# Preparing the first attention layer: loads of x, the first value product and the order of the pieces

## The chip, the cores and the metric

The kernel runs on one core of a Trainium2 chip. The metric is the device time of one execution in microseconds. TensorE (PE) multiplies, VectorE (DVE), ScalarE (ACT) and GpSimd (POOL) do element-wise work, and SyncE (SP) issues all DMA transfers of this kernel in the order of its queue.

## The reference

Four layers work in turn on one x of 2048 rows and 640 columns, in float32: attention, Fourier mixing, attention, Fourier mixing. Cut to what matters here:

```python
def attention(x, wqkv, wo):                      # H = 32 heads of 20, window W = 256
    q, k, v = split(x @ wqkv)                    # each (H, S, 20)
    scores = einsum("bhqd,bhkd->bhqk", q, k) * 20 ** -0.5
    mask = (i - j >= 0) & (i - j < 256)
    p = softmax(where(mask, scores, -1e9))
    return merge(einsum("bhqk,bhkd->bhqd", p, v)) @ wo

x = x + attention(layernorm(x), wqkv, wo)
x = x + real_fourier(layernorm(x))
x = x + attention(layernorm(x), wqkv, wo)
x = x + real_fourier(layernorm(x))
```

## The kernel before

Every float32 product is made of three products of rounded operands: each operand is split into a high half (a rounding copy, on ScalarE) and a low half (the rest, a subtraction on VectorE or GpSimd), and high x high, high x low and low x high are added up in PSUM. `split` makes the two halves and `all3` issues the three products for each of the five blocks of 128 columns (KC = 5).

The change is in `before_heads`, which prepares an attention layer before the loop over the heads. It works on 16 tiles of 128 rows of x, four tiles to a block (`sb`). For tile t:

- `prep_load` issues the load of the tile (320 KB) on SyncE. In layer 0 the tiles 0 to 11 go to eight places in `tmp`, tiles 12 and later to the rotating buffers of `raw`.
- `prep_stats` computes mean and variance on VectorE, and 1/sqrt on GpSimd.
- `prep_norm` normalizes the tile in place on VectorE.
- `prep_turn` makes five transposes on PE (four into a bank of role x4, the fifth into role x1, which has one bank), and splits what comes out, from PSUM, into high (ScalarE) and low (VectorE) halves in `xnt`.
- `value(t)` makes the value product of the tile: two halves of 320 columns, each 15 products, copied by ScalarE and VectorE into a buffer `vst`, which is stored to DRAM for each pair of tiles.

`prep` does, for a running number r, the load of a tile ahead, the statistics of r + 2, the normalization of r + 1 and the turn of r. It is called once in each `value` and in some of the `pieces`.

`load_w` loads one of the five blocks of the value weights and splits it; `split_w(n)` runs n steps of these, two to a weight. `pieces(sb)` computes two pieces (chunks of 128 query and key columns, 15 products of 512 columns each) for a block and stores them in DRAM (`qk_d`). `packed(sb)` issues the 12 loads that bring the queries and keys of the first four heads back in the layout of the heads. `values(sb)` is four calls of `value`.

What sets the order is the order of the Python code: each engine runs its instructions in the order in which they are issued there, and waits only for data and buffers. Nothing plans. The same holds for SyncE, on which a store that waits for its data holds up each load behind it. The layers 0 and 2 share the code; `first` marks layer 0.

In layer 0 the order on PE is, with V for a value product, P for a piece's 15 products and T for the turn of a tile: T0 T1 V0 T2 V1 T3 V2 T4 V3 T5 T6 P T7 and so on: two pieces of block 0 and two of block 1, then V4 to V7, pieces of block 2, V8 to V11, pieces of block 3, V12 to V15. After that the heads start, on line 553.

Of the kernel before, what the change touches and what calls it, by code (L numbers as in the profile page):

```python
# [17 lines left out]
P = 128  # L18
S = 2048
D = 640  # L20
KC = D // P
# [33 lines left out]
def cuts(ap, n):  # L55

    return [ap[:, i:i + n] for i in range(0, ap.shape[1] - n + 1, n)]


def pairs(c):  # L60
    return [(c[2 * i], c[2 * i + 1]) for i in range(len(c) // 2)]


class Net:
    def __init__(self, nc, tc, ctx, a):
        self.nc, self.tc, self.a = nc, tc, a
        const = ctx.enter_context(tc.tile_pool(name="const", bufs=1))
        self.ln = ctx.enter_context(tc.tile_pool(name="ln", bufs=5))
        self.slots = ctx.enter_context(tc.tile_pool(name="slots", bufs=1))
        psum = ctx.enter_context(tc.tile_pool(name="psum", bufs=1, space=PSUM))  # L70
        self.work = ctx.enter_context(tc.tile_pool(name="work", bufs=2))
        dram = ctx.enter_context(tc.tile_pool(name="dram", bufs=1, space=DRAM))

        self.banks = psum.tile([P, 8, 512], F32, name="banks")

        def fixed(name, cols, dt):
            return const.tile([P, cols], dt, name=name)

        self.ident = fixed("ident", P, F32)
        nc.sync.dma_start(self.ident, a["ident"])  # L80
        self.mask = fixed("mask", 384, BF16)
        self.ones = const.tile([1, 128], F32, name="ones")
        nc.vector.memset(self.ones, 1.0)
        self.half = fixed("half", 1, F32)
        nc.vector.memset(self.half, -0.5)
        self.big, self.home = [None] * 4, [0, 1, 2, 3]
        self.qp, self.kp = [None] * 2, [None] * 2

        self.qk = dram.tile([2, 2 * D, S], F32, name="qk_d")
        self.vd = dram.tile([NQ, P, NB, 96], F32, name="v_d")  # L90
        self.ud = dram.tile([2, KC, P, S], F32, name="u_d")
        self.od = dram.tile([H, 32, S], F32, name="o_d")
        self.rd = dram.tile([NSB, H, 512], F32, name="r_d")
        self.td = dram.tile([2, KC, P, D], F32, name="t_d")
        self.xs = [dram.tile([S, D], F32, name=f"x_d{i}") for i in range(3)]
        self.turn = {}
        self.xn = {}
        self.ready, self.hid = 0, False
        self.slot = None
        self.posted = {}  # L100
        self.heavy = []
        self.left = 0
        self.tmp = None
# [27 lines left out]
    def next(self, name):  # L131
        i = self.turn.get(name, 0)
        self.turn[name] = i + 1
        tiles = getattr(self, name)[:3]
        return tiles[i % len(tiles)]
# [164 lines left out]
    def before_heads(self, xsrc):  # L300
        nc, a = self.nc, self.a
        self.proj = self.project()
        ready = self.ready
        first = ready == 0
        vst = [t.rearrange("p (q t c) -> p q t c", t=2, c=96) for t in self.pt[:2]]
        for v in self.pt[:2]:
            (nc.vector if first else nc.gpsimd).memset(v, 1.0)
        if first:
            self.take_tmp()
        if first:  # L310
            for t in range(3):
                self.prep_load(xsrc, t)
        state = [ready, ready + (6 if first else 4)]
        wv = pairs(cuts(self.kp[1], D) + cuts(self.qp[1], D))[:KC]
        spare = (cuts(self.pt[2], D) + cuts(self.pt[3], D) if first else [None] * 4) + [None]
        wl = [self.load_w(wv, a["wv"], [k], at=k, eng=nc.vector if first and k > 2 else nc.gpsimd, into=spare[k])
              for k in range(KC)]
        for f in wl:
            next(f)
        if first:  # L320
            for t in range(3, 6):
                self.prep_load(xsrc, t)
                if t < 5:
                    self.load_chunk(t - 3)
            mask = self.raw()[:, :384]
            nc.sync.dma_start(mask, a["mask"])
        if first:
            self.prep_stats(0)
        self.prep_stats(ready + 1)
        if first:  # L330
            self.prep_norm(0)

        def prep():
            r = state[0]
            if state[1] < r + 5:
                self.prep_load(xsrc, state[1])
                state[1] += 1
            self.prep_stats(r + 2)
            self.prep_norm(r + 1)
            self.prep_turn(r)  # L340
            state[0] += 1

        def split_w(n):
            for _ in range(n):
                if wl and next(wl[0], 1) is not None:
                    wl.pop(0)

        def pieces(sb):
            for c in range(2):
                if first and sb == 0:  # L350
                    prep()
                self.piece(c, sb, "q")
                split_w(4)
                if ready or sb and state[0] < 4 * sb + 8:
                    prep()

        def value(t):
            v, xt = vst[t // 2 % 2], self.xnt(t // 4)
            rs = slice((t % 4) * P, (t % 4 + 1) * P)
            ps = []  # L360
            for hf in range(2):
                p = self.bank("v", 320)
                cs = slice(hf * 320, (hf + 1) * 320)
                self.all3(p, [((xt[:, 0, k, rs], xt[:, 1, k, rs]), (wv[k][0][:, cs], wv[k][1][:, cs]))
                              for k in range(KC)])
                ps.append(p)
            prep()
            for hf in range(2):
                dst = v[:, 4 * hf:4 * hf + 4, t % 2, 0:84].rearrange("p q (h c) -> p q h c", c=21)[:, :, :, 1:21]
                src = ps[hf].rearrange("p (q h c) -> p q h c", q=4, h=4)  # L370
                if hf == 0:
                    nc.scalar.activation(dst, src, AF.Copy)
                else:
                    nc.vector.tensor_copy(dst, src)  # L374
            if t % 2:
                nc.sync.dma_start(self.vd[:, :, t - 1:t + 1, :].rearrange("q p t c -> p q (t c)"),
                                  v.rearrange("p q t c -> p q (t c)"))

        def values(sb):
            for f in wl:  # L380
                for _ in f:
                    pass
            for i in range(4):
                value(4 * sb + i)

        def packed(sb):
            for f in self.pack(0, sb):
                f()

        if first:  # L390
            split_w(4)
            prep()
            split_w(6)
            prep()
            for t in range(4):
                if t in (1, 2):
                    self.cut_chunk(t - 1)
                value(t)
            nc.gpsimd.tensor_copy(self.mask, mask)
            pieces(0)  # L400
            pieces(1)
        else:
            pieces(0)
            pieces(1)
            values(0)
        self.take_qk("kp", 0)
        self.ones_rows(0)
        packed(0)
        packed(1)
        values(1)  # L410
        pieces(2)
        self.load_chunk(2)
        packed(2)
        values(2)
        pieces(3)
        self.cut_chunk(2)
        self.load_chunk(3)
        packed(3)
        values(3)
        self.ones_rows(1)  # L420
# [1309 lines left out]
```

## Time and profile before

| | |
|---|---|
| median of three runs | 2174.63 us (2174.54 to 2177.93) |
| the profiled execution | 2173.64 us |
| its span | 2171.9 us |
| first transpose on PE | 7.96 us after the span's start |
| first product of the heads on PE | 125.02 us |
| PE busy in the first 125 us | 112.06 us |

Times in the timeline count from the start of the span. A row of it gives start, duration, engine, line, operation, the tiles written and read, their form, and how many instructions in a row it stands for; in brackets is the idle time ahead of it and what ended it. Tiles are named by their buffers: `big` holds x tiles at first (the `tmp` places) and normalized, turned x; `kp` and `qp` hold the split value weights for a time; `pt` the raw weights 0 to 3 and the value buffers.

### The profile page before, as it was taken

Reading aid. Unit: us, or ns where it says so; the run is one execution under the profiler, and the core shown is the slowest. Engines: PE = TensorE matmul, PEld = TensorE weight load, DVE = VectorE, ACT = ScalarE, POOL = GpSimd, SP = SyncE. Lnnn points to the kernel's source line nnn. Section 1 sums busy time; section 2 is a strip of 40 time slices with the busy share of each in tenths; the row PEclk is TensorE's granted clock in tenths of the full one; section 3 lists DMA queues with packets and bytes.
Section 4 is the critical chain, followed back from the end, with each engine's and each line's share of the span. In section 5 each row is a group of like instructions: output and inputs, shape, how many; then the busy total and the mean of one; then the engine's idle time right before and its main releaser. Section 6 shows DMA issues by size and latency. Waiting matters only on the chain.

```text
span 2171.9 us, 49261 instructions
## 1 busy us (share of the span) xinstructions
PE 2116.4 (97%) x17893; PEld 1768.5 (81%) x17893; DVE 1611.6 (74%) x3933; ACT 1167.9 (54%) x2611; POOL 932.6 (43%) x1458
## 2 busy tenths in 40 slices
PE   7999999899999999999999999998999999999999
PEld 7987777687878888889999877776777788888899
DVE  6348888786897968787751578887768878688777
ACT  3117887766554545543431288786665545455522
POOL 3037777876514224230230477777754333242300
PEclk9999999999999999999999999999999999999999
DMA  5546666786435353657646466667853454546653
GB/s 184 177 146 198 203 190 212 218 233 200 135 122 180 132 187 126 224 196 258 214 140 189 152 201 187 207 193 224 233 184 130 130 189 136 165 148 218 221 176 125
DMA packets 221619, 395.41 MB, mean 182 GB/s; under 512 B 39360, under 2 KB 85952, under 8 KB 221376
## 3 DMA queue, kind: packets, MB, share of 16 engines
q1 hardware_dynamic: 221376, 392.26, 57.0%
q8 instruction: 141, 2.31, 0.5%
q14 instruction: 102, 0.84, 0.1%
HBM read 273.94 MB, written 117.05 MB: 180 GB/s over the span
## 4 chain that ended last, share of the span: by engine, by line
PE 81%; DVE 6%; POOL 4%; ACT 4%; DMA 3%; issue 2%; SPq 0%; ACTq 0%; POOLq 0%; DVEq 0%
PE banks L1269 27%; PE banks L173 14%; PE banks L191 13%; PE banks L613 8%; PE banks L1524 6%; PE banks L583 6%; PE banks L553 4%; POOL ou L1199 1%; POOL big L166 1%; DVE qp L166 1%; ACT big L931 1%; PE banks L273 1%; PE banks L565 1%; POOL rs L981 1%; ACT big L160 1%
## 5 line engine op out<-in xcount | busy, mean ns | idle before, releaser
L558 DVE CUSTOM_DVE_ANT_0 banks<-banks,mask 128x384 f32<-128x384 f32 (+2 forms) x1024 | 525.5, 559 | 153.4 <-PE banks L553 117.5
L592 ACT ACTIVATE pt<-banks 128x384 f32<-128x384 f32 (+2 forms) x1024 | 430.1, 472 | 139.8 <-PE banks L553 59.5
L583 PE MATMUL banks<-qp,kp 61*128 61x384 f32 (+2 forms) x1024 | 302.8, 365 | 9.7 <-DMA qp<-mt 7.7
L598 POOL TENSOR_SCALAR_AFFINE_SELECT pt<-pt 128x256 f32<-128x256 f32 x512 | 213.5, 418 | 174.9 <-ACT pt L592 128.4
L553 PE MATMUL banks<-kp,qp 60*128 60x384 f32 (+2 forms) x1024 | 279.1, 359 | 4.8 <-DVE mc L558 4.5
L191 PE MATMUL banks<-big,wc 64*128 64x512 f32 x1920 | 272.1, 394 | 0.4 <-DVE pt L374 0.4
L583 PEld LDWEIGHTS banks<-qp,kp 61*128 61x128 f32 x1024 | 176.8, 185 | 68.0 <-issue 27.4
L613 PE MATMUL banks<-pt,vq 128*32 128x128 f32 x5760 | 215.3, 277 | 4.4 <-POOL pt L598 4.4
L191 PEld LDWEIGHTS banks<-big,wc 64*128 64x128 f32 x1920 | 183.3, 185 | 29.1 <-ACT x L477 6.7
L613 PEld LDWEIGHTS banks<-pt,vq 128*32 128x32 f32 x5760 | 144.3, 109 | 65.2 <-issue 48.2
L1199 POOL TENSOR_TENSOR pt<-pt,pt 128x512 f32<-128x512 f32 x36 | 62.8, 1744 | 293.0 <-DMA pt<-c 188.3
L602 POOL TENSOR_SCALAR_AFFINE_SELECT pt<-pt 128x256 f32<-128x256 f32 x448 | 187.4, 418 | 0.0
L553 PEld LDWEIGHTS banks<-kp,qp 60*128 60x128 f32 x1024 | 163.7, 185 | 26.7 <-DVE mc L558 16.3
L160 ACT ACTIVATE c<-pt 128x512 fp32r<-128x512 f32 x150 | 93.5, 626 | 151.0 <-POOL pt L1175 52.4
L160 ACT ACTIVATE qp<-pt 128x512 fp32r<-128x512 f32 (+1 forms) x195 | 119.9, 624 | 92.2 <-DVE pt L1200 38.9
L166 DVE TENSOR_TENSOR c<-pt,c 128x512 fp32r<-128x512 f32 x150 | 125.0, 843 | 52.0 <-ACT c L160 49.8
L166 DVE TENSOR_TENSOR qp<-pt,qp 128x512 fp32r<-128x512 f32 (+1 forms) x195 | 150.2, 783 | 12.4 <-ACT qp L160 9.8
L1269 PE MATMUL banks<-qp,big 128*128 128x512 f32 x630 | 151.2, 391 | 4.9 <-DVE qp L166 3.9
L558 DVE DVE_READ_ACCUMULATOR2_ANT mc<- 128x1 f32 x1024 | 145.2, 142 | 0.0
L1269 PEld LDWEIGHTS banks<-qp,big 128*128 128x128 f32 x630 | 117.0, 188 | 31.0 <-DVE qp L166 5.6
L1269 PE MATMUL banks<-qp,xc 128*128 128x512 f32 x480 | 117.9, 390 | 1.5 <-DVE xc L166 1.2
L1269 PEld LDWEIGHTS banks<-qp,xc 128*128 128x128 f32 x480 | 89.8, 188 | 21.9 <-DVE xc L166 2.1
(224 smaller groups left out, 4388.6 us busy)
## 6 DMA issues: line engine op xcount, KB each, us to landing
pt<-c SPq DMA_DIRECT2D x188, 512.0 KB
qk_d<-c SPq DMA_DIRECT2D x80, 512.0 KB
kp<-qk_d SPq DMA_DIRECT2D x384, 80.0 KB
qp<-qk_d SPq DMA_DIRECT2D x384, 80.0 KB
kp<-u_d SPq DMA_DIRECT2D x32, 640.0 KB
o_d<-ou SPq DMA_DIRECT2D x64, 256.0 KB
x_d<-x SPq DMA_DIRECT2D x48, 320.0 KB
v_d<-pt SPq DMA_DIRECT2D x16, 768.0 KB
```

The lines of the kernel that those rows point to most:

```text
L160: nc.scalar.activation(hi, src, AF.Copy, scale=-1.0 if neg else 1.0)
L166: (eng or nc.vector).tensor_tensor(out=lo, in0=src, in1=hi.bitcast(F32), op=OP.subtract)
L173: self.nc.tensor.matmul(p, x, y, start=n == 0, stop=n == last)
L191: self.nc.tensor.matmul(ps[a], x[r], y[r], start=half + i == 0, stop=half == 1 and i == n - 1, skip_group_check=True)
L553: nc.tensor.matmul(p, qp[quad % 2][b:b + 60, z, qb * P:(qb + 1) * P], kp[quad % 2][b:b + 60, z, k0 * P:(qb + 1) * P], start=True, stop=True)
L558: nc.vector.tensor_tensor_reduce(out=p, in0=p, in1=self.mask[:, 384 - n * P:], scale=1.0, scalar=NEG, op0=OP.add, op1=OP.max, accum_out=mc ...
L583: nc.tensor.matmul(self.banks[:, tb[e], :n * P], kp[quad % 2][b:b + 61, z, kb * P:(kb + 1) * P], qp[quad % 2][b:b + 61, z, kb * P:(kb + n) ...
L592: nc.scalar.activation(pt[quad, kb][:, 2 * z + e, :n * P], self.banks[:, tb[e], :n * P], AF.Exp, scale=SCALE)
L598: nc.gpsimd.affine_select(out=t[:, :, 0:P], in_=t[:, :, 0:P], pattern=[[0, 2], [1, P]], compare_op=OP.is_ge, fill=0.0, base=0, channel_mul ...
L602: nc.gpsimd.affine_select(out=t[:, :, 256:384], in_=t[:, :, 256:384], pattern=[[0, 2], [-1, P]], compare_op=OP.is_gt, fill=0.0, base=0, ch ...
L613: nc.tensor.matmul(p[32 * h:32 * h + 32, :], vq[:, 96 * (kb % 4) + 21 * h:96 * (kb % 4) + 21 * h + 32], t[:, h, (qb - kb) * P:(qb - kb + 1 ...
L1269: nc.tensor.matmul(self.banks[:, bk, :], p, b[q], start=start and m == 0, stop=stop and last and m == 2, skip_group_check=True)
```

## The change

In layer 0, `before_heads` is written in another order:

- Tile 0 of x is loaded first, then the identity for the transposes, the five weights, and tiles 1 to 7, with the two chunks of query and key weights and the mask between them. Before, tiles 0 to 2 stood ahead of the weights. `prep` now loads tile r + 6 (before, r + 4 at most), so the load of a tile stands further ahead in SyncE's queue.
- The low halves of all five value weights are made on VectorE. Before, those of weights 0 to 2 were made on GpSimd.
- A new function `opening` takes the place of the first steps: statistics, normalization and turn of tile 0 with the weights' splits between them, and the normalization of tile 1.
- A new function `first_value` makes the first value product: for each of the five blocks k it issues the three products of both halves, where `all3` makes one half through all blocks and then the other. The turn of tile 1 stands in it ahead of block 3.
- The turn of tile r then stands behind V r-1, one step later than before, up to V3. The first two pieces have no call of `prep` ahead of them any more.
- Pieces of block 1 come after V4 to V7, and V8 to V11 come ahead of the pieces of block 2.

The diff:

```diff
-        nc.sync.dma_start(self.ident, a["ident"])
@@ before_heads
         if first:
-            for t in range(3):
-                self.prep_load(xsrc, t)
-        state = [ready, ready + (6 if first else 4)]
+            self.prep_load(xsrc, 0)
+            nc.sync.dma_start(self.ident, a["ident"])
+        state = [2, 8] if first else [ready, ready + 4]
...
-        wl = [self.load_w(wv, a["wv"], [k], at=k, eng=nc.vector if first and k > 2 else nc.gpsimd, into=spare[k])
+        wl = [self.load_w(wv, a["wv"], [k], at=k, eng=nc.vector if first else nc.gpsimd, into=spare[k])
               for k in range(KC)]
...
         if first:
-            for t in range(3, 6):
+            for t in range(1, 8):
                 self.prep_load(xsrc, t)
-                if t < 5:
-                    self.load_chunk(t - 3)
-            mask = self.raw()[:, :384]
-            nc.sync.dma_start(mask, a["mask"])
-        if first:
-            self.prep_stats(0)
-        self.prep_stats(ready + 1)
-        if first:
-            self.prep_norm(0)
+                if t in (3, 5):
+                    self.load_chunk(t // 2 - 1)
+                if t == 4:
+                    mask = self.raw()[:, :384]
+                    nc.sync.dma_start(mask, a["mask"])
+        else:
+            self.prep_stats(ready + 1)
@@ prep
-            if state[1] < r + 5:
+            if state[1] < r + (8 if first else 5):
@@ pieces
-                if first and sb == 0:
-                    prep()
                 self.piece(c, sb, "q")
                 split_w(4)
-                if ready or sb and state[0] < 4 * sb + 8:
+                if ready or state[0] < 4 * sb + 9:
                     prep()
+        def opening():
+            self.prep_stats(0)
+            self.prep_norm(0)
+            split_w(6)
+            self.prep_turn(0)
+            self.prep_stats(1)
+            split_w(2)
+            self.prep_norm(1)
+            split_w(2)
+
+        def first_value(ps):
+            xt = self.xnt(0)
+            for k in range(KC):
+                if k == 3:
+                    self.prep_turn(1)
+                for hf, p in enumerate(ps):
+                    cs = slice(hf * 320, (hf + 1) * 320)
+                    for a, b in ((0, 0), (0, 1), (1, 0)):
+                        nc.tensor.matmul(p, xt[:, a, k, :P], wv[k][b][:, cs], start=k + a + b == 0,
+                                         stop=k == KC - 1 and a == 1)
+            self.prep_stats(2)
+            self.prep_norm(2)
+            self.prep_stats(3)
@@ value
-            prep()
+                prep()
+            else:
+                first_value(ps)
@@ the end of before_heads
         if first:
-            split_w(4)
-            prep()
-            split_w(6)
-            prep()
+            opening()
             for t in range(4):
                 if t in (1, 2):
                     self.cut_chunk(t - 1)
                 value(t)
             nc.gpsimd.tensor_copy(self.mask, mask)
             pieces(0)
-            pieces(1)
...
         packed(0)
-        packed(1)
-        values(1)
+        if first:
+            values(1)
+            pieces(1)
+            packed(1)
+            values(2)
+        else:
+            packed(1)
+            values(1)
         pieces(2)
...
-        values(2)
+        if not first:
+            values(2)
         pieces(3)
```

How the instructions move, on PE from the first transposes to the second value product. L273 and L272 are the transposes of an x tile, five to a turn, L173 and L172 value products out of `all3`, L370 those of `first_value`; `kp` holds weights 0 to 2, `qp` weights 3 and 4. Before:

```order
L273 MATMUL banks<-ident,big_108 128x128 x10
L173 MATMUL banks<-kp_103,big_157 128x320 x9
L173 MATMUL banks<-qp_104,big_157 128x320 x6
L173 MATMUL banks<-kp_103,big_157 128x320 x9
L173 MATMUL banks<-qp_104,big_157 128x320 x6
L273 MATMUL banks<-ident,big_108 128x128 x5
```

Now:

```order
L272 MATMUL banks<-ident,big_107 128x128 x5
L370 MATMUL banks<-kp_102,big_144 128x320 x18
L272 MATMUL banks<-ident,big_107 128x128 x5
L370 MATMUL banks<-qp_103,big_144 128x320 x12
L172 MATMUL banks<-kp_102,big_144 128x320 x9
L172 MATMUL banks<-qp_103,big_144 128x320 x6
```

The second turn has moved into the first value product, behind its first 18 products, and the third turn from before the second value product to behind it.

On VectorE, the opening: L218 and L217 with the two lines after them are a tile's statistics, L236 and L235 a normalization, L166 and L165 low halves, out of `pt` or `x` those of a weight, out of `banks` those of a turned tile. Before, after the two fills:

```order
L218 BN_STATS st<-big_108 128x6 x2
L220 BN_AGGR mv<-st 128x2
L222 TENSOR_SCALAR rs<-mv 128x1
L218 BN_STATS st<-big_108 128x6 x2
L220 BN_AGGR mv<-st 128x2
L222 TENSOR_SCALAR rs<-mv 128x1
L236 TENSOR_SCALAR big_108<-big_108,mv,rs 128x640
```

Now:

```order
L217 BN_STATS st<-big_107 128x6 x2
L219 BN_AGGR mv<-st 128x2
L221 TENSOR_SCALAR rs<-mv 128x1
L235 TENSOR_SCALAR big_107<-big_107,mv,rs 128x640
L165 TENSOR_TENSOR kp_102<-pt_95,kp_102 128x640 x2
L165 TENSOR_TENSOR kp_102<-pt_96,kp_102 128x640
L165 TENSOR_TENSOR big_144<-banks,big_144 128x4x128
L165 TENSOR_TENSOR big_144<-banks,big_144 128x128
```

The normalization of tile 0 has moved ahead of the statistics of tile 1, and three weights' low halves stand between it and tile 0's own low half.

On SyncE, the queue around the first loads of queries and keys (L250 and L249 are loads of x, L456 and L479 piece stores, L424 and L447 the rows of ones, L510 and L533 the loads of `packed`). Before:

```order
L456 DMA qk_d<-c 128x2x512
L250 DMA x<-x 128x640
L424 DMA kp_560<-ones 1x32x128 x2
L510 DMA kp_560<-qk_d 20x2x512 x6
L510 DMA qp_105<-qk_d 20x2x512 x6
L510 DMA kp_560<-qk_d 20x2x512 x6
L510 DMA qp_105<-qk_d 20x2x512 x6
L250 DMA x<-x 128x640 x2
```

Now:

```order
L479 DMA qk_d<-c 128x2x512
L249 DMA x<-x 128x640
L447 DMA kp_465<-ones 1x32x128 x2
L533 DMA kp_465<-qk_d 20x2x512 x6
L533 DMA qp_104<-qk_d 20x2x512 x6
L249 DMA x<-x 128x640 x2
```

The two loads of x behind the queries and keys are tiles 14 and 15 before and 13 and 14 now, and twelve loads fewer stand ahead of them; block 1's twelve come later, behind its pieces.

More of the change, by code (lines that the diff above doesn't have):

```diff
@@ L359, in value @@
             rs = slice((t % 4) * P, (t % 4 + 1) * P)
[L360 to L366, printed above, removed]
-            prep()
+            ps = [self.bank("v", 320) for _ in range(2)]
+            if t or not first:
+                for hf, p in enumerate(ps):
+                    cs = slice(hf * 320, (hf + 1) * 320)
+                    self.all3(p, [((xt[:, 0, k, rs], xt[:, 1, k, rs]), (wv[k][0][:, cs], wv[k][1][:, cs]))
+                                  for k in range(KC)])
+                prep()
+            else:
+                first_value(ps)
             for hf in range(2):
```

## The prediction

> **What bounds the kernel now.** The page comes first: which engine fills the span, and which carries the chain of work that ended last.
>
> ```profile
> span 2171.9 us, 49261 instructions
> PE 2116.4 (97%) x17893; PEld 1768.5 (81%) x17893; DVE 1611.6 (74%) x3933; ACT 1167.9 (54%) x2611; POOL 932.6 (43%) x1458
> PE 81%; DVE 6%; POOL 4%; ACT 4%; DMA 3%; issue 2%; SPq 0%; ACTq 0%; POOLq 0%; DVEq 0%
> ```
>
> TensorE (PE) is busy for 97% of the span and carries 81% of the chain. The change touches only the preparation of layer 0, so the second view is the busy time by stretches of that preparation. Columns: the stretch, its length, busy time of PE, weight loads, VectorE, ScalarE, GpSimd, granted clock, DMA share, GB/s.
>
> ```profile
> 0.00:8.00 8.00, 0.04 (x1) 0.04 (x1) 5.94 (x14) 1.28 (x1) 1.30 (x6) 1.00 0.70 214
> 8.00:16.00 8.00, 5.32 (x19) 4.12 (x20) 6.44 (x15) 4.66 (x9) 6.98 (x6) 1.00 1.04 399
> 16.00:24.00 8.00, 8.00 (x46) 8.00 (x45) 4.03 (x12) 1.72 (x4) 1.65 (x3) 1.00 0.09 34
> 35.50:58.00 22.50, 21.43 (x119) 18.56 (x118) 14.84 (x38) 6.22 (x15) 3.59 (x6) 1.00 0.58 186
> 74.00:125.00 51.00, 50.86 (x315) 47.92 (x315) 13.08 (x28) 9.35 (x21) 2.14 (x3) 1.00 0.49 158
> ```
>
> PE does nothing for 8 us and 5.3 of the next 8; after 74 us it is full. The third view says what PE waited for until the heads start (start, us, engine, line, operation; then the wait table).
>
> ```profile
> PE banks L273 <- DVE big L236: 8.4, 2, 8.0
> PE banks L273 <- DVE big L166: 1.7, 2, 1.1
> PE banks L173 <- POOL kp L166: 1.6, 1, 1.6
> PE banks L273 <- DVE x L236: 1.1, 1, 1.1
> ...
> 125.02 0.33 PE L553 MATMUL banks<-kp,qp 60*128 60x128 f32 x2
> ```
>
> Four waits: the first normalized tile (to 7.96 us), GpSimd's low half of a weight, a copy out of PSUM, a late tile. A fifth loss shows only in the PE timeline, whose rows time every step:
>
> ```profile
> 7.96 1.33 PE L273 MATMUL banks<-ident,big 128*128 128x128 f32 x5 [7.96 <-DVE big L236]
> 11.62 2.21 PE L173 MATMUL banks<-kp,big 128*128 128x320 f32 x7
> 15.43 0.90 PE L173 MATMUL banks<-kp,big 128*128 128x320 f32 x2 [1.60 <-POOL kp L166]
> 17.73 2.46 PE L173 MATMUL banks<-kp,big 128*128 128x320 f32 x9
> 20.04 1.04 PE L173 MATMUL banks<-qp,big 128*128 128x320 f32 x6
> 20.91 0.71 PE L273 MATMUL banks<-ident,big 128*128 128x128 f32 x5
> 21.38 1.56 PE L173 MATMUL banks<-kp,big 128*128 128x320 f32 x9
> 25.85 0.71 PE L273 MATMUL banks<-ident,big 128*128 128x128 f32 x5
> 35.74 1.15 PE L273 MATMUL banks<-ident,big 128*128 128x128 f32 x9
> 37.95 0.33 PE L273 MATMUL banks<-ident,big 128*128 128x128 f32 x1 [1.07 <-DVE big L166]
> 38.04 3.70 PE L173 MATMUL banks<-big,wc 128*128 128x512 f32 x15
> 41.58 0.71 PE L273 MATMUL banks<-ident,big 128*128 128x128 f32 x5
> 73.98 1.13 PE L273 MATMUL banks<-ident,x 128*128 128x128 f32 x5 [1.08 <-DVE x L236]
> ```
>
> Nine products of 320 columns take 2.46 us from 17.73 and step every 0.267 us; the same nine take 1.56 from 21.38, a step of 0.147 (a whole value product with one tile's turn lasts from 20.91 to 25.85, 4.94, so 4.47 for the product and 0.47 for the turn). The array ran at about half pace until some 4.4 us after it resumed at 15.43, though the granted clock in the windows is 1.00 throughout. I write V for a value product, P for a piece, "turn" for the five transposes of an x tile.
>
> **The change, part by part.** All times are those of the profiled execution.
>
> *The opening, turn 0 to V0.* Rows of the other engines give the prices:
>
> ```profile
> 2.94 1.34 DVE L307 MEMSET pt<- 128x1536 f32 x1 [0.27 <-issue]
> 5.64 0.55 POOL L225 TENSOR_TENSOR rs<-rs,half 128x1 f32<-128x1 f32 x1 [5.14 <-DVE rs L222]
> 6.06 0.89 DVE L218 BATCH_NORM_STATS2 st<-big 128x6 f32<-128x320 f32 x2 [0.50 <-DMA big<-x]
> 7.30 0.60 DVE L236 TENSOR_SCALAR big<-big,mv,rs 128x640 f32<-128x640 f32 x1
> 8.52 1.51 ACT L160 ACTIVATE kp<-pt 128x640 fp32r<-128x640 f32 x2 [6.44 <-DMA pt<-wv]
> 9.33 3.24 POOL L166 TENSOR_TENSOR kp<-pt,kp 128x640 fp32r<-128x640 f32 x2 [1.02 <-DMA pt<-wv]
> 13.17 0.81 DVE L166 TENSOR_TENSOR qp<-x,qp 128x640 fp32r<-128x640 f32 x1
> 26.49 0.77 ACT L160 ACTIVATE big<-banks 128x512 fp32r<-128x512 f32 x2 [3.23 <-PE banks L273]
> 27.12 0.89 DVE L166 TENSOR_TENSOR big<-banks,big 128x512 fp32r<-128x512 f32 x2 [1.84 <-ACT big L160]
> L225 POOL TENSOR_TENSOR rs<-rs,half 128x1 f32<-128x1 f32 x16 | 12.8, 802 | 47.2 <-DVE rs L222 47.2
> ```
>
> Tile 0's statistics still wait for the two fills (2.94 + 1.34). Its root on GpSimd ends at 5.64 + 0.55 = 6.19, and the normalization no longer sits behind tile 1's statistics: it starts near 6.2 instead of 7.30, and turn 0 at 6.9 instead of 7.96. The weights move two places up in the DMA queue. Tile 1 landed at 6.06 (it ended VectorE's wait), the first weight at 8.52 (ScalarE's), with tile 2 between them, so 1.23 us a transfer there; later ones at the 399 GB/s of the second window take 0.82 for 328 KB. So weights 0, 1, 2 land at about 6.05, 7.3, 8.5, weights 3 and 4 at 9.3 and 10.1, tile 1 at 10.9. The third weight decides: ScalarE's high half 0.74 (half of 1.51), VectorE's low half 0.81 and only then, next in VectorE's row, tile 0's low half: 8.5 + 0.75 + 0.85 = 10.1, and 0.6 more for the first four blocks, so 10.75. V0's third product needs it. From there 16 products at 0.267 and 0.15 for the restart end at 15.2. Turn 1 and the last twelve products must then be ready: tile 1's statistics 10.9 to 12.3 (as 0.89 and two small steps), root 0.80 to 13.1, normalization to 13.8, weight 4's low half to 14.6. They are, with 0.6 to spare, and with the low halves on VectorE (0.81 each, for 1.6 on GpSimd) the wait at 15.43 is gone. If full pace comes as before 4.4 us after the unbroken start, at 15.2, the rest takes 0.47 + 12 x 0.147 + 0.1 = 2.3: V0 ends at 17.5. Turn 2 moves behind V1; for equal work I add its 0.47: 18.0 against 21.38, **a gain of 3.4 us**. Bounds: full pace from 14.3 gives 17.1; none inside V0 gives 15.2 + 5 x 0.213 + 12 x 0.267 = 19.5 (0.213 is 7.96's pace, five in 1.07). That is 3.8 to 1.4.
>
> [...]
>
> *A new wait before V2 and V3.* Before, turn t+1 stood ahead of V t. Now turn 2 stands directly ahead of V2 and turn 3 ahead of V3, so PE waits for the copies of the tile it has just turned. From 25.85, the turn ends at 26.32; the high copy starts at 26.49 and the low one at 27.12, its four-block half done 0.6 later: 1.4 from the turn's end to the third product, which otherwise starts 0.37 after it. **Loss 1.05 for V3.** At V2 VectorE is also late: after tile 1's low half (17.3) it has tile 2's statistics 1.3, the wait for its root 0.8, a normalization 0.6, statistics of tile 3 1.3, V0's copy 0.4, statistics of tile 4 1.3 and normalization 0.6 ahead of turn 2's low half: 23.6, usable at 24.2; V1 and turn 2 end on PE at 22.5. **Loss 1.3 for V2.** V4 and later have two turns in hand, so nothing there. Bounds for the two: 2.0 (V3's price twice) to 3.4 (VectorE half a us later at both).
>
> *The doubled turn goes.* From 35.74 to 38.04, 2.30 us, PE made turns 5 and 6 in one run; the tenth transpose at 37.95 waited for VectorE to empty the single bank of the fifth block. Two turns cost 0.94. Now a piece or a product stands between any two turns from V1 on: **gain 1.35**. It is hidden again only if VectorE needs over the 3.5 us of a piece between turns (38.04 to 41.58); its rows for one (0.69, 1.3, 0.6, 0.9) make that 3.5, so 0 to 0.2 a piece could come back.
>
> *Loads ahead of stores.* Tile 14 came late:
>
> ```profile
> 67.88 1.71 SPq L250 DMA_DIRECT2D x<-x  x2
> 72.08 0.89 DVE L218 BATCH_NORM_STATS2 st<-x 128x6 f32<-128x320 f32 x2 [6.68 <-DMA x<-x]
> ...
> 113.09 2.79 SPq L510 DMA_DIRECT2D qp<-qk_d  x6
> ```
>
> Its load was issued at 67.88, behind the 24 key and query loads of two blocks; VectorE's statistics waited 6.68 us, PE 1.1 (the wait table). Now tiles 13 and 14 stand behind the loads of block 0 alone, some 12 loads or 5.5 us earlier in the queue, and block 0's are themselves needed no sooner; by the rows' pace the loads go out near 52 and are first read near 69. **Gain 1.1**; bounds 0.9 to 1.1.
>
> *Pieces later, V8 to V11 ahead of P of block 2.* The same products in another order: nothing. Block 1's twelve loads now go ahead of V8's store, and the P of blocks 2 and 3 run as 60 products in a row, with the third block's loads between their stores on SyncE. What hides it: V12 to V15, 4 x 4.4 = 17.6 us of PE work behind the last piece, against the 8 to 9 us by which block 3's loads (the row of 113.09, over at 115.88) trailed the last piece before, and some 6 for the block now ahead of them; if that cover went, the heads would wait for these loads one for one. From the first row of the heads on, the order is the same.
>
> **Sum**: 3.4 - 2.35 + 1.35 + 1.1 = 3.5 us. The profiled execution took 2173.64 (its span 2171.9 and 1.7 around it), so **2170.1**. The median of the runs shown is 2174.63, 1 us above it; from there it would be 2171.1. What a measurement of this kernel can tell from no change is about 0.2%, 4.35 us, so faster by that means under 2170.28: the forecast lies on the edge. The terms' bounds (1.4 to 3.8, -2.0 to -3.4, 1.0 to 1.35, 0.9 to 1.1) give gains of 0 to 4.2, mostly 2.5 to 4.2: 2169.4 to 2171.2.
>
> **Rivals.**
> *The new waits cost nothing.* If V2's and V3's turns are hidden (PE's queue or a faster VectorE), the 2.35 stays: gain 5.9, 2167.8. For it: VectorE idles before low copies in many rows. Against: products 1 to 3 of a tile need its low half, whatever the queue.
> *The opening is bound by the array's pace.* V0 at half pace throughout ends at 19.5: gain 1.5, 2172.1. For it: before, pace rose only after 4.4 us unbroken, and here the stream has a break after two products. Against: those breaks lie before 10.75.
> *Slower: the waits at V2 and V3 drop the array to half pace.* Place: the 1.4 us and 1.7 us gaps. Price: 60 products at 0.267 for 0.147, 7.2 us, and a turn 0.6: 3.5 - 7.8, 2177.9. It decides from the point where a gap of about 1.5 us is enough. Against: the gap of 1.34 us before 37.95 was followed at once by 15 products in 3.70, the full pace.
> *Slower: tile 1 late.* It now queues behind five weights, and turn 1 stands inside V0. Slack 0.6 to 1.4 us; every us beyond delays all of PE one for one, so slower than before from 5 us late, landing at 16; at 9 late 2179. For it: the first window moved only 214 GB/s. Against: the second window's 399.
> *The loads do not come ahead*, because SyncE still stalls on a store: gain 2.4, 2171.2, inside the forecast's range.
>
> **How the numbers follow.** The sum as worked out 0.50, of which 0.30 under the edge of 2170.28 and 0.20 above; the waits hidden 0.18, faster; half pace in V0 0.17, same; half pace at V2 and V3 0.08, of which 0.03 same; tile 1 late 0.07, slower. Faster 0.48, same 0.40, slower 0.12. The time is that of the likeliest, 2170.1. Eight in ten: from below the hidden waits' 2167.8 less half a us to above the half-pace case and the runs' own 1 us, 2167.2 to 2174.6; the two slower cases are left out.
>
> **What would show it.** Turn 0 at 6.9; the third product of V0 near 10.75 after a wait on VectorE; no wait on GpSimd's low half at all; V0 over near 17.5; waits of over 1 us ahead of V2 and V3, on ScalarE and VectorE; single turns of 0.71 with no gap between V3 and V4; VectorE never waiting for an x tile after 40 us; the heads' first product near 121.5 for 125.02, and the rest of the span unmoved. A first head later than 123, or a gap at turn 1, makes the prediction wrong; so does a span that changes by another amount than the first head's start.

## The result and the profile after

The changed kernel took 2171.11 us (median of 14 runs, 2167.74 to 2172.6) against 2174.59 (14 runs) before: a ratio of 0.9981, 95% interval 0.9974 to 0.9989, 3.5 us faster. In a second comparison on another occasion it was 0.9989 (0.9980 to 0.9997). The forecast was a gain of 3.5 us and a time of 2170.1, or 2171.1 counted from the median before. It called a time "faster" only under 2170.28, on the ground that less than about 0.2% cannot be told from no change. The median stayed above that edge, yet the interval lies clear of 1: here a smaller change could be told.

The profiled execution took 2169.7 us for 2173.64. Its span, the wait table of PE up to the heads, and the first product of the heads (start, us, engine, line, operation):

```profile
span 2168.0 us, 49263 instructions
PE banks L272 <- DVE big L235: 6.8, 1, 6.8
PE banks L370 <- ACT big L159: 2.4, 1, 2.4
PE banks L172 <- ACT big L159: 1.2, 2, 0.6
PE banks L172 <- DVE big L165: 0.7, 2, 0.5
...
121.24 0.33 PE L576 MATMUL banks<-kp,qp 60*128 60x128 f32 x2
```

The span is 3.9 us shorter and the heads start 3.78 us earlier (125.02 before); what lies behind the heads' start is 2046.9 us before and 2046.8 now. So the gain was made entirely ahead of the heads. The wait on GpSimd's low half, the doubled turn's and the late tile's are gone; new are two pairs of waits ahead of V2 and V3, and one of 2.4 us ahead of V0. That one is for the high copy of tile 0, which ScalarE makes only behind the high halves of weights 1 and 2 (8.40 to 9.93). The PE timeline of the changed kernel shows them (L370 are the products of `first_value`):

```profile
6.78 1.33 PE L272 MATMUL banks<-ident,big 128*128 128x128 f32 x5 [6.78 <-DVE big L235]
10.47 4.69 PE L370 MATMUL banks<-kp,big 128*128 128x320 f32 x18 [2.36 <-ACT big L159]
15.00 0.71 PE L272 MATMUL banks<-ident,big 128*128 128x128 f32 x5
15.46 2.00 PE L370 MATMUL banks<-qp,big 128*128 128x320 f32 x12
17.30 1.48 PE L172 MATMUL banks<-kp,big 128*128 128x320 f32 x9
21.70 0.71 PE L272 MATMUL banks<-ident,big 128*128 128x128 f32 x5
22.98 0.56 PE L172 MATMUL banks<-kp,big 128*128 128x320 f32 x2 [0.58 <-ACT big L159]
24.05 1.29 PE L172 MATMUL banks<-kp,big 128*128 128x320 f32 x7 [0.50 <-DVE big L165]
28.26 0.71 PE L272 MATMUL banks<-ident,big 128*128 128x128 f32 x5
29.54 0.56 PE L172 MATMUL banks<-kp,big 128*128 128x320 f32 x2 [0.58 <-ACT big L159]
30.27 1.29 PE L172 MATMUL banks<-kp,big 128*128 128x320 f32 x7 [0.16 <-DVE big L165]
34.47 0.71 PE L272 MATMUL banks<-ident,big 128*128 128x128 f32 x5
42.91 1.56 PE L172 MATMUL banks<-kp,big 128*128 128x320 f32 x9
```

V0 is over at 17.30, where V1 starts. From 21.70 a turn of 0.47 ends at 22.17; V2's first two products run at 22.98, the third only at 24.05, 1.9 us after the turn for the 0.37 of an undisturbed product. V3's third comes 1.5 after its turn (28.26, 30.27). From 34.47 on single turns follow without a gap.

Where a run is compared by the heads' start below, that is because the part behind it came out between 2045.4 and 2049.3 us in the thirteen profiles of this study. In each of them PE waits there for one DMA near 420 us and for another near 1500 us, 2.5 to 5.4 and 3.6 to 5.9 us long. A single time cannot tell one us, the heads' start can; that the two profiles above agree to 0.1 us behind the heads is luck.

### The profile page after: what moved, and what is told of

It is laid out like the page before. It is cut to its first block, busy times and chain, and to the rows that moved or that the text cites. A ratio compares the mean times of both kernels' runs of the same rounds, so it can differ in the third digit from the quotient of the medians.

```text
span 2168.0 us, 49263 instructions
## 1 busy us (share of the span) xinstructions
PE 2114.2 (98%) x17893; PEld 1765.7 (81%) x17893; DVE 1613.7 (74%) x3936; ACT 1167.3 (54%) x2611; POOL 923.4 (43%) x1455
## 4 chain that ended last, share of the span: by engine, by line
PE 84%; DVE 5%; POOL 4%; ACT 4%; DMA 2%; issue 1%; SPq 0%; ACTq 0%; DVEq 0%; POOLq 0%
PE banks L1292 29%; PE banks L172 15%; PE banks L190 14%; PE banks L636 8%; PE banks L1547 6%; PE banks L606 6%; PE banks L576 4%; POOL big L165 1%; ACT big L954 1%; PE banks L272 1%; DVE qp L165 1%; POOL ou L1222 1%; PE banks L588 1%; POOL rs L1004 1%; ACT big L159 1%
## 5 line engine op out<-in xcount | busy, mean ns | idle before, releaser
L621 POOL TENSOR_SCALAR_AFFINE_SELECT pt<-pt 128x256 f32<-128x256 f32 x512 | 210.1, 411 | 178.1 <-ACT pt L615 130.2
L625 POOL TENSOR_SCALAR_AFFINE_SELECT pt<-pt 128x256 f32<-128x256 f32 x448 | 184.1, 411 | 0.0
L165 DVE TENSOR_TENSOR c<-pt,c 128x512 fp32r<-128x512 f32 x150 | 122.3, 825 | 50.6 <-ACT c L159 48.4
L165 DVE TENSOR_TENSOR qp<-pt,qp 128x512 fp32r<-128x512 f32 (+1 forms) x195 | 150.7, 786 | 12.3 <-ACT qp L159 9.6
```

The source lines that it names most:

```text
L165: (eng or nc.vector).tensor_tensor(out=lo, in0=src, in1=hi.bitcast(F32), op=OP.subtract)
L621: nc.gpsimd.affine_select(out=t[:, :, 0:P], in_=t[:, :, 0:P], pattern=[[0, 2], [1, P]], compare_op=OP.is_ge, fill=0.0, base=0, channel_mul ...
L625: nc.gpsimd.affine_select(out=t[:, :, 256:384], in_=t[:, :, 256:384], pattern=[[0, 2], [-1, P]], compare_op=OP.is_gt, fill=0.0, base=0, ch ...
```

## The experiments

The first eight change one thing each, seven in the changed kernel and one in the kernel before, with one execution profiled.

**Turns 2 and 3 half a product earlier.**

```diff
+                early = first and t in (1, 2)
                 for hf, p in enumerate(ps):
                     cs = slice(hf * 320, (hf + 1) * 320)
+                    if early and hf:
+                        self.prep_turn(state[0])
                     self.all3(p, ...)
-                prep()
+                prep(not early)     # False: the turn is left out of prep
```

> The changed kernel with turns 2 and 3 moved forward by half a value product: turn 2 stands between the two halves of V1, turn 3 between those of V2, so that each tile's copies run beside 15 products of the tile before. My theory: the waits ahead of V2 and V3 in the changed kernel (third product at 24.05 after a turn from 21.70, and at 30.27 after one from 28.26) come from the turn's place alone, and both go: first product of the heads at 121.24 - 1.5 - 1.2 = 118.5 us. The rival: VectorE's chain (statistics and normalizations behind V0) is what V2 waits for, and then the wait only moves into V1 or V2, with the heads no earlier than 120.2.

The heads started at 119.28, 1.96 earlier, and PE's wait table has no row left for V2 and V3. V0 had ended at 17.96 in this execution, 0.66 later than in the changed kernel's, so the waits themselves are worth 2.6. The theory holds; they came from the place of the turn.

**The low halves of weights 0 to 2 on GpSimd again.**

```diff
-  eng=nc.vector if first else nc.gpsimd
+  eng=nc.vector if first and k > 2 else nc.gpsimd
```

> The changed kernel with the low halves of weights 0 to 2 on GpSimd again. My prediction's step: the low halves on VectorE are what ended the wait of 1.6 us for GpSimd, so the wait comes back and the heads start 1 to 1.6 later, at 122.2 to 122.8 us. The rival: V0 through the blocks with its halves in turn needs weight 2 only after 12 products, some 3.2 us later at half pace, so GpSimd's 1.6 us for each is hidden, VectorE reaches tile 0's low half sooner, and the heads start between 120.9 and 121.3.

121.03 us, and no wait of PE for GpSimd in the table: the rival had the time right. The move of the low halves to VectorE is not what the end of the 1.6 us wait needed. GpSimd's rows tell why, first of the kernel before, then of this run (L225 is the root of a tile, L166 and L165 are low halves):

```profile
12.53 1.13 POOL L225 TENSOR_TENSOR rs<-rs,half 128x1 f32<-128x1 f32 x1
13.63 1.75 POOL L166 TENSOR_TENSOR kp<-pt,kp 128x640 fp32r<-128x640 f32 x1
```

```profile
6.50 1.61 POOL L165 TENSOR_TENSOR kp<-pt,kp 128x640 fp32r<-128x640 f32 x1 [0.43 <-ACT kp L159]
8.70 3.05 POOL L165 TENSOR_TENSOR kp<-pt,kp 128x640 fp32r<-128x640 f32 x2 [0.58 <-DMA pt<-wv]
```

Before, the third weight's low half ended at 15.38, behind the root of tile 2. Here the three run without a root between them, and the third ends at 11.75. V0's third product ran at 10.69; with one half after the other its eighth, the first that needs this low half, would come near 12.2 (an estimate at 0.267 a step). So the rival's reason, the halves in turn, was not needed for this wait either.

**V0 one half after the other.**

```diff
-            for k in range(KC):
-                if k == 3:
-                    self.prep_turn(1)
-                for hf, p in enumerate(ps):
+            for hf, p in enumerate(ps):
+                for k in range(KC):
+                    if k == 3 and hf == 0:
+                        self.prep_turn(1)
```

> The changed kernel with V0 made one half after the other, as all the other value products; turn 1 still stands ahead of block 3 of the first half. My theory: PE reaches turn 1 after 9 products for 18, near 13.5 us, and waits there for tile 1's normalization, which ends at 14.8 in the changed kernel, and then for the low half of weight 4 (15.5): V0 ends near 18.7 for 17.3, the heads start at 122.6. The rival: V0 is bound by the pace of the array, not by the order of its products, and the heads stay at 121.2 within 0.4.

The heads started at 123.05, 1.8 later. In its PE timeline turn 1 waits for tile 1's normalization behind nine products, as expected, and V0 ends at 19.44:

```profile
9.66 3.21 PE L370 MATMUL banks<-kp,big 128*128 128x320 f32 x9 [1.55 <-ACT big L159]
14.01 1.33 PE L272 MATMUL banks<-ident,big 128*128 128x128 f32 x5 [1.14 <-DVE big L235]
14.99 1.95 PE L370 MATMUL banks<-qp,big 128*128 128x320 f32 x6
16.74 1.98 PE L370 MATMUL banks<-kp,big 128*128 128x320 f32 x9
19.44 1.48 PE L172 MATMUL banks<-kp,big 128*128 128x320 f32 x9
```

With the halves in turn, twice as many products stand ahead of turn 1, and that hides tile 1's normalization. The array also stayed at half pace until 17.9 here, for 13.9 in the changed kernel, so the 1.8 us are more than the wait of 1.14. No wait for a weight's low half came back: V0's eighth product ran at 12.14 without a gap, in the old order of products. So the 1.6 us wait stays away with the low halves on either engine, and, by this run and the estimate above, with either order of V0's products. What the rows leave is that the low halves start earlier and stand together in their engine's row; which of the two it took was not tried apart.

**The old order of the pieces.**

```diff
             pieces(0)
+            prep()
+            pieces(1)
...
-        if first:
-            values(1)
-            pieces(1)
-            packed(1)
-            values(2)
-        else:
-            packed(1)
-            values(1)
+        packed(1)
+        values(1)
         pieces(2)
...
-        if not first:
-            values(2)
+        values(2)
```

> The changed kernel with the old order of pieces: those of block 1 right behind those of block 0, and V8 to V11 behind the pieces of block 2; the loads keep their new lead. Since turns stand one step later than before, block 1's pieces need one turn more ahead of them, so turns 6 and 7 come in one run. My theory: the doubled turn costs its 1.3 us again, no tile of x is late, and the heads start at 122.6. The rival: it is the pieces' place and not the loads' lead that keeps tiles 13 to 15 in time, and a wait on a load of x adds about 1 us: 123.6.

129.99 us: 8.75 later, far beyond both. No wait of VectorE for a load of x is in its tables, so the loads' lead alone kept the tiles in time and the rival falls; but the doubled turn cost much more than 1.3. Its PE timeline:

```profile
43.93 0.71 PE L272 MATMUL banks<-ident,big 128*128 128x128 f32 x5
47.25 1.27 PE L272 MATMUL banks<-ident,big 128*128 128x128 f32 x5 [2.61 <-DVE big L235]
48.72 0.79 PE L172 MATMUL banks<-big,wc 128*128 128x512 f32 x1 [0.21 <-ACT big L159]
50.39 5.37 PE L172 MATMUL banks<-big,wc 128*128 128x512 f32 x14 [0.87 <-DVE big L165]
55.59 0.71 PE L272 MATMUL banks<-ident,big 128*128 128x128 f32 x5
56.06 3.69 PE L172 MATMUL banks<-big,wc 128*128 128x512 f32 x15
```

Turn 7 waited 2.6 us for its normalization, which VectorE reached late, the first piece of block 1 needed that very tile and waited twice more, and 14 of its products then took 5.37 us where fifteen take 3.69 at 56.06. From the end of turn 6 at 44.4, a turn and a piece would be done at 48.4; they were at 55.6. That is 7.2 of the 8.75; the rest is V0, which ended 1.5 later here. So the new order of the pieces is what makes turns one step later affordable: it puts four value products between the pieces of block 0 and those of block 1.

**The loads ahead, alone, in the kernel before.**

```diff
-        state = [ready, ready + (6 if first else 4)]
+        state = [ready, ready + (8 if first else 4)]
-            for t in range(3, 6):
+            for t in range(3, 8):
-                if t < 5:
+                if t in (3, 4):
-            if state[1] < r + 5:
+            if state[1] < r + (7 if first else 5):
```

> The kernel before with the loads of x ahead alone: tiles 6 and 7 are loaded with the first six, and from then on tile r + 6 is loaded in the preparation step r, so that tiles 14 and 15 stand ahead of the loads of queries and keys. My theory: VectorE's wait of 6.7 us for tile 14 and with it PE's 1.1 us go, and nothing else moves: the heads start at 123.9 us for 125.02. The rival: the loads ahead collide with stores or other loads and the wait moves to another place: no earlier than 124.8.

122.50 us, 2.5 earlier. Row by row against the kernel before, turn 2 stood 0.83 earlier already (20.08 for 20.91, an opening in which transfers landed and the pace rose sooner), still so at the next run of pieces (41.19 for 42.04). The turn that had waited at 73.98 came at 71.85, and the heads 2.52 earlier: the late tile was worth 1.7, not 1.1: beside PE's wait for the tile, the turn's last transpose at 74.78 in the kernel before came another 0.4 late.

**The old lead of the loads, in the changed kernel.**

```diff
-            if state[1] < r + (8 if first else 5):
+            if state[1] < r + 5:
```

> The changed kernel with the old lead of the loads (tile r + 4 at most in step r); pieces and products stay in the new order. My prediction gave the 1.1 us of the late tile to the loads: then a tile of 12 to 15 is late again, and the heads start near 122.3 us for 121.24. The rival: block 1's twelve loads now come behind V4 to V7, so no tile stands behind 24 loads whatever its lead, and the new order of pieces is enough: 121.2, apart from when the array takes up its full pace (in the five profiles so far its slow stretch ended 3.3 to 6.3 us after the first product of V0, worth up to 1.5 us of the heads' start).

121.38 us for 121.24: no loss. VectorE waited once for a load of x, 2.6 us near 57.6, and PE not at all. Loads ahead and pieces later each cure the late tile, and the second needs no help from the first.

**The array kept busy ahead of V0.** A function `idle(n)` makes n transposes of the identity into a PSUM bank, and nobody reads them; `idle(13)` stands ahead of turn 0, `idle(12)` behind it.

> The changed kernel with 25 transposes of the identity added on PE that nothing reads: 13 ahead of turn 0, from the identity's landing near 4 us, and 12 behind it. My theory: the half pace is that of an array that has been idle, so the pace rises before V0, and V0 is then bound by the third weight's low half (first long run of products from 11.4) and by tile 1's normalization (turn 1 at 14.8): V0 ends at 17.0 to 17.3 in every execution, where it ended between 17.05 and 18.8 in the profiles so far. The rival: transposes do not count as work for the pace, and V0 starts at half pace (steps of 0.267) and ends between 17.3 and 18.8.

```profile
4.10 3.04 PE L354 MATMUL banks<-ident 128*128 128x128 f32 x13 [4.10 <-DMA ident<-ident]
6.93 1.02 PE L272 MATMUL banks<-ident,big 128*128 128x128 f32 x5
7.78 1.47 PE L354 MATMUL banks<-ident 128*128 128x128 f32 x12
11.12 2.61 PE L376 MATMUL banks<-kp,big 128*128 128x320 f32 x16 [0.42 <-DVE big L165]
14.51 0.77 PE L272 MATMUL banks<-ident,big 128*128 128x128 f32 x5 [0.78 <-DVE big L235]
16.88 1.48 PE L172 MATMUL banks<-kp,big 128*128 128x320 f32 x9
```

The transposes step at 0.213 from 4.10 and at 0.109 from 7.6 on (twelve now take 1.47), and V0's products at 0.147 from 11.37: sixteen in 2.61 us. V0 then waited 0.78 for tile 1 and ended at 16.88, the heads started at 120.85. The theory holds in this execution.

**Tiles 1 and 2 ahead of the weights again.**

```diff
-            self.prep_load(xsrc, 0)
+            for t in range(3):
+                self.prep_load(xsrc, t)
...
-            for t in range(1, 8):
+            for t in range(3, 8):
```

> The changed kernel with tiles 1 and 2 ahead of the weights in the DMA queue, as before the change. My prediction's step: the third weight's low half decides the start of V0, so its landing two transfers of 0.8 us later moves V0's third product from 11.44 to 13.1 us and the heads to 122.8. The rival: tile 1, which landed at 11.6 behind the weights, decides the opening through turn 1, and with it early the heads stay within 0.4 of 121.2.

Neither. The heads came at 122.54, but V0's third product at 11.35, as in the changed kernel (11.44): the pace rose late here (products at half pace until 16.6, V0 over at 18.67), and that is the 1.3 us. ScalarE's high halves tell when the weights landed, first of the changed kernel, then of this one:

```profile
6.10 0.74 ACT L159 ACTIVATE kp<-pt 128x640 fp32r<-128x640 f32 x1 [4.02 <-DMA pt<-wv]
8.40 1.53 ACT L159 ACTIVATE kp<-pt 128x640 fp32r<-128x640 f32 x2 [1.56 <-DMA pt<-wv]
```

```profile
7.49 2.34 ACT L159 ACTIVATE kp<-pt 128x640 fp32r<-128x640 f32 x3 [5.41 <-DMA pt<-wv]
```

The first weight landed at 6.1 and the second only at 8.4 in the one; in the other the first at 7.5, and all three high halves run through by 9.8, with the third at 9.1 as against 9.2. That does not show that two transfers of 328 KB ahead of the weights are free. This execution moved 275 GB/s up to 9.1 us, the other twelve profiles 222 to 249. The landing of the third weight in all traces tells more: with the tiles ahead it is 10.09 in the kernel before, 9.83 with the loads alone, 10.03 in the last version below and 9.07 here; with the weights ahead it lies between 8.2 and 9.3 in nine profiles. By these the two tiles cost it about 1 us.

**The better version**, in two steps, timed in five rounds beside the changed kernel itself.

> The changed kernel itself, for comparison on the same chip: 3.5 us under the kernel before (ratio 0.998), and the heads between 121.0 and 122.5 us, by when the array takes up its full pace.

> The changed kernel with both edits that helped: turns 2 and 3 between the halves of V1 and V2, and the 25 unread transposes ahead of V0. My theory: the two do not overlap, the first removes 2.7 us of waits ahead of V2 and V3, the second puts V0's end at 16.9, so the heads start at 120.85 - 2.7 = 118.2 us and the time is 3 us under the changed kernel's. The rival: with V0 over sooner, VectorE's chain (statistics and normalization of tiles 2 and 3) holds turn 2, and the heads start at 119 or later.

> As the last one, with the opening in another order: tiles 1 and 2 are loaded ahead of the weights again (which cost V0 nothing), tile 1's statistics are made while VectorE waits for the first weight, turn 0's low half comes before those of weights 1 and 2, turn 1 ahead of block 2, with 18 unread transposes. My theory: V0 is then bound by the weights' low halves in turn, starts near 9.7 and ends near 15.2 for 16.9, and the heads start at 118.2 - 1.7 = 116.5 us. The rival: the weights land later behind the two tiles, or VectorE's low halves queue up, and V0 ends no earlier than 16.5: heads at 117.8 or later.

The edit of the last, beside that of the first experiment:

```diff
             nc.sync.dma_start(self.ident, a["ident"])
+            for t in range(1, 3):
+                self.prep_load(xsrc, t)
...
             self.prep_stats(0)
             self.prep_norm(0)
-            split_w(6)
-            self.prep_turn(0)
             self.prep_stats(1)
             split_w(2)
-            self.prep_norm(1)
+            idle(12)
+            self.prep_turn(0)
+            idle(6)
             split_w(2)
+            self.prep_norm(1)
+            split_w(6)
...
-                if k == 3:
+                if k == 2:
                     self.prep_turn(1)
```

| | time, us | ratio to the kernel before | V0 over | heads start |
|---|---|---|---|---|
| changed kernel | 2171.4 | 0.9989 (0.9980 to 0.9997) | 17.60 | 121.59 |
| turns inside, array busy | 2167.52 | 0.9972 (0.9962 to 0.9982) | 16.19 | 117.57 |
| and the opening reordered | 2165.1 | 0.9964 (0.9950 to 0.9977) | 15.22 | 116.26 |

Both theories held, within 0.7 us of the heads' start. The last version's PE timeline has no wait of over 0.3 us between 4.11 and the heads:

```profile
4.11 2.82 PE L357 MATMUL banks<-ident 128*128 128x128 f32 x12 [4.11 <-DMA ident<-ident]
6.77 1.33 PE L272 MATMUL banks<-ident,big 128*128 128x128 f32 x5
10.26 1.93 PE L379 MATMUL banks<-kp,big 128*128 128x320 f32 x10 [0.18 <-DVE big L165]
13.46 1.92 PE L379 MATMUL banks<-qp,big 128*128 128x320 f32 x12
15.22 1.48 PE L172 MATMUL banks<-kp,big 128*128 128x320 f32 x9
17.42 0.71 PE L272 MATMUL banks<-ident,big 128*128 128x128 f32 x5
17.88 1.56 PE L172 MATMUL banks<-kp,big 128*128 128x320 f32 x9
116.26 0.33 PE L588 MATMUL banks<-kp,qp 60*128 60x128 f32 x2
```

It beats both kernels: 8.35 us under the one before in this comparison. The third weight landed late in it, at 10.0, but V0 needs that weight only from its thirteenth product on (12.50), and the wait ahead of V0 shrank from 2.4 to 0.3 us, since tile 0's copies no longer stand behind the third weight. How much of the last step came from the turn 0 moved ahead of two weights, and how much from tile 1's earlier statistics, was not tried apart.

## Why the prediction was right, and where it was not

The forecast of the size was right, and so was most of the place: the heads start at 121.24 for a predicted 121.5, and the rest of the span did not move. Term by term:

- *The opening*, predicted 3.4: V0 over at 17.30, with turn 2's 0.47 17.8 against 21.38, is 3.6. Two errors in it cancelled. The third weight's chain was late: weight 2 landed at 9.2 for 8.5, and V0's third product came at 11.44 for 10.75. The pace rose early: at 13.9, 3.4 us after V0's first product, where the working took 15.2. The bound of 3.8 took full pace from 14.3, a time for which the trace before has no figure; in the changed kernel the record of the clock begins at 13.90. In the five profiles with this very opening V0 ended between 17.30 and 18.77, so that the size came out so exactly is luck.
- *The cause in the opening* was right in part. "With the low halves on VectorE the wait at 15.43 is gone": it is gone, but with GpSimd too, so the engine was not what it took. "The weights move two places up": the third landed at 9.17 for 10.09 in the kernel before, 0.9 earlier where the working had 1.6.
- *The granted clock* was taken at its word. It is 1.00 in the windows of the opening only because the traces hold no record of it there: all thirteen profiles read 1.00 from 0 to 16 us, slow products and all, in the traces of the two kernels the record begins only when the pace rises (19.89 before, 13.90 now), and a window without a record counts as 1.00. Where the record covers a slow stretch, it reads 0.50 (426.08 to 429.49 in the kernel before).
- *The waits ahead of V2 and V3*, predicted 1.3 and 1.05: 1.5 and 1.2, by the rows (24.05 and 30.27, less 0.37 after the turn's end). The mechanism was as described, down to VectorE being late at V2 only. Removing them gave 2.6.
- *The doubled turn*, 1.35: gone, no wait for PSUM is left in the table. Its price in the other order is not 1.35 but 7.2, when the tile it turns is needed at once.
- *The late tile*, 1.1: mis-sized, 1.7 in the kernel before with the loads alone, since only PE's first wait was counted, not what the late turn delayed behind it.
- *Pieces later: nothing*: right as a sum, wrong as a judgement. Without this edit the others lose 7.2 us.

The terms as measured, 3.6 - 2.7 + 1.35 + 1.7, make 4.0 for the 3.78 by which the heads moved. Of the rivals, half pace at V2 and V3 did not happen: gaps of 0.8 us left V2 to V3 at 0.147 a product. Half pace all through V0 did not happen in this execution, though in two others (the old pieces, tiles first) only the last twelve products of V0 ran faster; their V0 ended at 18.8 and 18.7. That spread of 1.5 us between executions is of the size of the difference between the sum and the two measured gains (3.5 and 2.1 us). Tile 1 was late, 11.63 for 10.9, but normalized at 14.78, 0.2 ahead of turn 1; where the pace rose sooner turn 1 waited for it, 0.78 with the array kept busy.

The stretches at half clock that the traces of the two kernels record in full last 3.41 us (from 426.08 before and 423.50 now) and 6.83 us (from 1501.28 and 1498.70). In the seven profiles of the changed kernel and its variants whose V0 ran on in one stream from its third product, the slow stretch ended between 3.3 and 6.6 us after V0's first product (13.90 less 10.47, 3.4, in the changed kernel): no fixed time fits them. My fixed 4.4 us had one execution behind it (15.43 to 19.89); in the run with the loads alone, on the same opening, it was 3.5.

## What to carry to other kernels

When an edit moves a tile's preparation to just ahead of its use, look for half a product's worth of other work to put between: that was worth 2.6 us here. Let a product run through its inner blocks for all its outputs in turn while its operands are still landing; it doubles the number of products that stand ahead of each late operand. And test the parts of a bundle one at a time: here one part did nothing, two parts were two cures for one wait, and one that "does nothing" held the rest up.

## What the runs showed of the hardware

- The array's half pace came back, and the granted clock showed it. With the old pieces PE waited 2.61 us ahead of turn 7 and another 0.87 ahead of 50.39; the 14 products of 512 columns from there took 5.37 us, where fifteen took 3.69 at 56.06. The granted clock is 0.85 over the 22.5 us from 35.50 to 58.00 in that run (1.00 in the changed kernel), which 6.8 us at 0.50 would make (an estimate). Behind the heads, in the kernel before, PE waited for a DMA for 2.87 us up to 426.35 and for 4.82 up to 1504.86, and the clock reads 0.50 for 3.41 us from 426.08 and for 6.83 from 1501.28. In the changed kernel the waits are 3.53 us up to 423.62 and 4.28 up to 1501.42, and the clock reads 0.50 for 3.41 us from 423.50 and for 6.83 from 1498.70. Gaps of 0.8 us in V2 and the idle 1.07 us ahead of 37.95 in the kernel before did not bring it back.
- Transposes raised the pace as products did: behind the unread ones, sixteen of V0's products took 2.61 us from 11.12. In the three runs that begin with unread transposes their step fell from 0.213 to 0.109 us 3.4, 4.9 and 4.3 us after the first.
- The early transfers moved more slowly than the later ones, and unevenly: between 4 and 5 us the core moved 113 GB/s in the changed kernel and 342 with the tiles first, from 9 to 12 us about 410 in both. Why the second weight took 2.3 us behind the first in the changed kernel, for 0.8 a transfer from 9 us on, stays open.
